# The last two late slots of a mixture-of-experts kernel as one mixed slot, and the third walk's first weights behind two conditional loads

## The chip, the cores and the metric

The kernel runs on one core of a Trainium2 chip. The metric is the device time of one execution in microseconds, the median of several runs. Of the engines, TensorE (PE) multiplies, VectorE (DVE) and ScalarE (ACT) work on the results, GpSimd (POOL) issues gathers and scatters, and SyncE (SP) issues loads and transposes by DMA, one after the other from one queue.

## The reference

Three stages run one after the other on 4608 tokens of width 512.

```python
k_p, v_p = k, v averaged over groups of 8 keys          # 8 batches, 8 heads, 576 queries, 72 keys
attn = softmax(scale * q @ k_p.T) @ v_p
h = x @ w_in                                            # 512 -> 2048
x = (max(h, 0) + alpha * min(h, 0)) @ w_out             # 2048 -> 512
expert = argmax(x @ w_gate)                             # 8 experts, one for each token
out[t] = gate[t] * (max(x[t] @ w1[e], 0) @ w2[e])       # e = expert[t], 512 -> 1024 -> 512
```

The tokens of an expert are known only at run time. With the inputs of this case the experts hold 537, 0, 1152, 576, 615, 576, 576 and 576 tokens.

## The kernel before

Float32 products are made of 16-bit parts: each operand is split into a high and a low half, and three matmuls (high·high, high·low, low·high) stand for one product. The operations of the first stages and of most of the last are given to a planner with a key (a due time) each; it fixes one order for each engine by keys, by which operation must wait for which, and by buffers that are taken and given back. The order is then written out as it stands.

The expert stage works in *slots* of up to 128 tokens of one expert. Slots 0 to 7 (the A slots) take tokens known early, 8 and up (the B slots) the rest. A slot goes through these steps: `tok` (ScalarE reads a row number into a register and loads the slot's token list, L1517), `gather` (GpSimd fetches the token rows, L1527), `xT` (SyncE transposes them, L1540), the first product `s1t` (24 matmuls of 512 columns, line `hp` L1561), ReLU on ScalarE (`rlt`), the split on VectorE (`hst`), two transposes on SyncE (`hT`, L1577), the second product `s2t` (24 matmuls, L1584), scaling on VectorE (`fin`, L1606 and L1608) and a scatter on GpSimd (`scat`, L1611).

The weights of a slot are held in one of three sets of buffers, the *walks*: A slots alternate between walks 0 and 1, B slots go over walks 0, 2, 1. `wload` (L1503 to L1511) issues a slot's weights on SyncE: `wload(0)` reads one or two registers and issues the pair of loads for the first product, `wload(1)` the pair for the second, 1 MB each. They are conditional: a slot whose walk already holds its expert skips the transfer, but the instructions stay in the queue. The first loads of a walk (slots 0, 1 and 9) are unconditional. Those of slot 9, the first on walk 2, wait in the plan for `oXt[5]`, the transpose of slot 5's tokens.

How many B slots there are is known only at run time; 31 with these inputs, so slot 38 is the last. Slots up to 36 are planned in full. From slot 37 on (`cond` = 38, `n >= cond - 1`) a slot's functions are kept in `tail`, and `run_tail` writes them out behind the plan, inside branches on the number of slots. These slots use `s1` (96 matmuls with the weights stationary and 128 token columns moving, L1552), whose result needs no transpose, and `s2` (48 matmuls for two slots, L1601). Slot 37's first product is still planned.

`plan_disp` sets up the tables for the B slots with small VectorE operations: `dB` (slots for each expert), `rows` and `rows2` (row numbers), `change` (which slot must load weights), `scales`.

Of the kernel before, what the change touches and what calls it, by code (L numbers as in the profile page):

```python
# [185 lines left out]
def attn_moe_moe_kernel(ctx: ExitStack, tc: tile.TileContext, q, k, v, w_in, w_out, alpha,  # L186
# [1165 lines left out]
    disp, cntA, cntB = {}, {}, {}  # L1352
    NW = (NSL - NA + 2) // 3

    def disp_0():
# [15 lines left out]
    def plan_disp(c, nm, key, o_cnt, o_c, o_inv):  # L1371
# [27 lines left out]
        def dB():  # L1399
            ni, nf, inc, off = t("ni", [128, NE], I32), t("nf", [128, NE]), t("inc", [128, NE]), t("off", [128, 1, NE])  # L1400
            V.scalar_tensor_tensor(out=nf, in0=cntA["u"], scalar=-128.0, in1=c["cp"], op0=ALU.mult, op1=ALU.add)
            V.tensor_scalar(out=ni, in0=nf, scalar1=127.0, scalar2=None, op0=ALU.add)
# [5 lines left out]
            ai, af = t("ai", [128, 2], I32), t("af", [128, 2])  # L1408
# [3 lines left out]
            V.tensor_copy(af, ai)  # L1412
            V.tensor_tensor(out=af[:, 0:1], in0=tot, in1=af[:, 0:1], op=ALU.subtract)
            V.tensor_scalar(out=jt[:, 2, :, 0], in0=jt[:, 0, :, 0], scalar1=1.0, scalar2=None, op0=ALU.add)
            V.tensor_scalar(out=jt[:, 1, :, 0], in0=jt[:, 2, :, 0], scalar1=af[:, 1:2], scalar2=None, op0=ALU.add)
            V.tensor_scalar(out=jt[:, 0, 1:, 0], in0=jt[:, 0, 1:, 0], scalar1=af[:, 0:1], scalar2=None, op0=ALU.add)
            V.tensor_copy(c["tot"], tot)
# [9 lines left out]
        def rows2():  # L1427
# [7 lines left out]
            if is_a:  # L1435
                V.scalar_tensor_tensor(out=regs[:, 0, :], in0=ej[:, :, 0], scalar=float(NT), in1=oj[:, :, 0],
                                       op0=ALU.mult, op1=ALU.add)
                return
            V.scalar_tensor_tensor(out=oj, in0=ej, scalar=float(NT), in1=oj, op0=ALU.mult, op1=ALU.add)
            oh, uj = t("oh", [128, n2, NE]), t("uj", [128, n2, 1])  # L1440
# [5 lines left out]
            V.scalar_tensor_tensor(out=regs[:, 0, :], in0=uj[:, :, 0], scalar=128.0, in1=oj[:, :, 0],  # L1446
                                   op0=ALU.mult, op1=ALU.add)

        def change():
# [10 lines left out]
        def scales():  # L1460
# [8 lines left out]
            V.tensor_tensor(out=ge, in0=c["oh"], in1=disp["wi"].to_broadcast([128, n2, NE]), op=ALU.mult)  # L1469
            V.tensor_reduce(out=sj, in_=ge, axis=AX.X, op=ALU.add)  # L1470

        o = counted[NB - NLAST] = add("PE", 0.1, count, [o_cnt], key=key, acq=[("gps", 1)])
        o = add("DVE", tiny(5 if is_a else 15), dA if is_a else dB, [o, o_c], key=key, rel=[("gps", 1)])
        o_w = add("DVE", tiny(4), rows, [o], key=key)
        o_r = add("DVE", tiny(5 if is_a else 10), rows2, [o_w], key=key)
        o_ch = add("DVE", tiny(2 if is_a else 5), change, [o_w], key=key + 0.1)
        o_s = add("DVE", tiny(6), scales, [o_r] + o_inv, key=key + 2)
# [4 lines left out]
    wbuf, oS1, oS2, oXt, oGa, last = {}, {}, {}, {}, {}, {}  # L1482
    tail, own = [], []

    def plan_slots(c0, lo, n_slots, oD, o_x2, o_tab, o_exp, base, cond):
# [3 lines left out]
        for i in range(n_slots):  # L1489
# [23 lines left out]

            def tok(s=s, c=c):
# [16 lines left out]
            def xT(c=c, n=n, tt=tt):  # L1531
                if n <= cond:
                    c["xT"] = wk.tile([128, 2 * KD, 128], F16, tag=tt, name="x2gT", bufs=2)
                else:
                    i = n - cond - 1
                    if i == 0:
                        own.extend(big([128, 2, 16, 128], F16, f"own{z}") for z in range(3))
                    c["ht"] = own[i // 2][:, i % 2].rearrange("p (z f) t -> p z f t", z=2)
                    c["xT"] = own[2].rearrange("p a (b f) t -> p (a b) f t", b=2)[:, i]
                Y.dma_start_transpose(out=c["xT"], in_=c["x2"])  # L1540

            def s1(f4, c=c, walk=walk):
                if "ht" not in c:
                    c["ht"] = wk.tile([128, 2, KF2, 128], F16, tag="eo", name="ht", bufs=2)
# [58 lines left out]

            def fin(s=s, c=c):
                cb = wk.tile([128, 1], F32, tag="cb", name="cb", bufs=2)
                V.tensor_tensor(out=cb, in0=c["rec"][:, 1:2], in1=c0["sj"][:, s, :], op=ALU.mult)  # L1606
                c["o"] = wk.tile([128, DM], F32, tag="q", name="so", bufs=3)
                V.tensor_scalar(out=c["o"], in0=c["op"], scalar1=cb, scalar2=None, op0=ALU.mult)  # L1608
# [4 lines left out]

            if n >= cond - 1:
                tail.append(((tok, gather, xT), wload, s1, rl, hs, s2, fin, scat))
            if n >= cond + 3:
                continue
            late = n == cond + 2
            d1 = d2 = []
# [10 lines left out]
            o_w1 = add("SP", 0.01 if rare else dmat(1 << 21), lambda f=wload: f(0), [o_w] + o_exp + d1, key=key - 14, acq=got)  # L1630
            if not late:
                o_w2 = add("SP", 0.01 if rare else dmat(1 << 21), lambda f=wload: f(1), [o_w1] + o_exp + d2, key=key - 13, acq=got)
            if n > cond + 1:
                continue
            if n == cond + 1:
# [5 lines left out]

            if n >= cond:
                continue
            hl = []
            if n < cond - 1:
                for f4 in range(KF2 // 4):
# [5 lines left out]
                    hl.append(add("SP", 1.0, lambda f=hT, f4=f4: f(f4), [o], order=hl[:], kind="xT", key=key - 20,  # L1652
                                  acq=[(th, 1)] if f4 == 0 else [], rel=[(tl, 1)]))
                o = oS2[n] = add("PE", pe(24, DM), s2t, hl + [o_w2], key=key + SLAG, acq=[("y", 1)], rel=[(th, 1)])
# [3 lines left out]
            for f4 in range(KF2 // 4):  # L1658
                o = oS1[n, f4] = add("PE", pe(48, 128), lambda f=s1, f4=f4: f(f4), [o_x, o_w1, oS1.get((n, f4 - 1))],
                                     key=key - 4.2 + 2 * f4, acq=[("h", 1)] + ([("eo", 1)] if f4 == 0 else []),  # L1660
                                     rel=[(tt, 1)] if f4 == KF2 // 4 - 1 else [])
                o = add("ACT", act(512), lambda f=rl, f4=f4: f(f4), [o], key=key - 2 + 2 * f4, acq=[("e", 1)], rel=[("h", 1)])
                hl.append(add("DVE", 0.5 + dve(512), lambda f=hs, f4=f4: f(f4), [o], key=key - 1 + 2 * f4, rel=[("e", 1)]))

    def run_tail():
# [3 lines left out]

        def up(k):  # L1670
            s1, rl, hs = tail[k][2:5]
            for f4 in range(KF2 // 4):
                s1(f4)
                rl(f4)
                hs(f4)

        def down(k):
            for f in tail[k][5:]:
                f()

        def step(k):
# [3 lines left out]
            with tc.If(total > NSL - NA - nt + 1 + k) as cmp:  # L1685
                if k + 3 < nt:
                    for f in tail[k + 3][0]:
                        f()
                up(k + 1)
                if k + 4 < nt:  # L1690
                    tail[k + 4][1](0)
                down(k)
                if k + 3 < nt:
                    tail[k + 3][1](1)
                step(k + 1)
            with cmp.Else():
                down(k)
        step(0)


# [66 lines left out]
```

## Time and profile before

| | us |
|---|---|
| three runs | 1320.1, 1323.67, 1324.22 (median 1323.67) |
| the profiled execution | 1320.55 |
| its span, first to last instruction | 1318.5 |
| mean granted TensorE clock | 0.981 |
| TensorE busy | 1266.5 (96%) |
| VectorE busy | 902.1 (68%) |
| ScalarE busy | 566.4 (43%) |
| GpSimd busy | 313.6 (24%) |

Times in rows count from the span's start. A share of busy time is a mean over all stages. The time of a matmul in a row (379 ns for 512 columns) runs from its issue to its modelled end, and matmuls overlap, so what a pass costs TensorE is the distance from its start to the next start. SPq, ACTq and POOLq are the queues in which an engine issues DMA; such a row shows how long the issue took, not the transfer. "x4" joins instructions that followed each other.

### The profile page before, as it was taken

What the parts mean: (1) busy time and instruction counts of PE and PEld (TensorE: products, weight loads), DVE (VectorE), ACT (ScalarE), POOL (GpSimd) and SP (SyncE); (2) the same over time, 40 slices, a digit from 0 to 9 for tenths busy, and PEclk for the clock granted to TensorE, in tenths of its full rate; (3) what the DMA queues carried; (4) which work ended last, traced back from release to release, by engine and by line L of the source; (5) the groups of instructions that cost most, each with busy time, mean ns of one, the idle gap of its engine ahead of it and who ended that gap; (6) DMA issues with size and microseconds to landing.
All of it is one profiled execution on the core that took longest, in us unless ns stands there. A gap on an engine that the chain in (4) does not pass through costs nothing. (4 is left out here: it accounts for less than half of the span.)

```text
span 1318.5 us, 25527 instructions
## 1 busy us (share of the span) xinstructions
PE 1266.5 (96%) x9181; PEld 785.3 (60%) x9181; DVE 902.1 (68%) x2206; ACT 566.4 (43%) x1316; POOL 313.6 (24%) x347
## 2 busy tenths in 40 slices
PE   4789999999999999999999999999989999999997
PEld 3677566677667667756776676674434444444454
DVE  4999888998999899889998887754423222323231
ACT  4887454565467447546665665431101111111110
POOL 2543432112231212123331211021121122122101
PEclk9689999999999999999999999999989999999999
DMA  9943696677788687797977665498778755999765
GB/s 269 352 123 88 164 246 161 160 196 188 168 201 196 164 200 194 162 206 199 258 201 170 181 193 154 95 310 194 221 177 196 159 128 151 253 252 210 152 191 183
DMA packets 374491, 252.64 MB, mean 192 GB/s; under 512 B 321927, under 2 KB 323095, under 8 KB 369752
## 3 DMA queue, kind: packets, MB, share of 16 engines
q1 hardware_dynamic: 360904, 230.67, 70.1%
q0 software_dynamic: 7552, 20.23, 5.0%
q8 instruction: 75, 1.23, 0.4%
q10 hardware_dynamic: 5904, 0.04, 0.3%
q14 instruction: 56, 0.46, 0.1%
HBM read 264.57 MB, written 54.87 MB: 242 GB/s over the span
## 5 line engine op out<-in xcount | busy, mean ns | idle before, releaser
L1066 PE MATMUL hp<-xT,w_in_hl 128*128 128x256 f16 x3456 | 392.4, 274 | 2.1 <-DVE r L1084 1.3
L1113 PE MATMUL yp<-w_out_hl,gT 128*128 128x512 f16 x1728 | 383.6, 379 | 1.6 <-DVE x L252 1.6
L1066 PEld LDWEIGHTS <-w_in_hl 128*128 128x128 f16 x3456 | 334.6, 98 | 46.7 <-issue 3.6
L1113 PEld LDWEIGHTS <-gT 128*128 128x128 f16 x1728 | 165.7, 98 | 192.2 <-issue 1.7
L1561 PE MATMUL hp<-ws,x2gT 128*128 128x512 f16 x888 | 199.7, 382 | 6.4 <-DMA ws<-wsc 5.5
L1566 ACT ACTIVATE hr<-hp 128x512 f32<-128x512 f32 x74 | 44.2, 597 | 324.4 <-PE hp L1561 304.0
L1561 PEld LDWEIGHTS <-x2gT 128*128 128x128 f16 x888 | 87.2, 98 | 113.2 <-DMA x2gT<-x2g 6.0
L1584 PE MATMUL op<-ws,hT 128*128 128x512 f16 x672 | 149.3, 379 | 0.0
L1084 DVE SCALAR_TENSOR_TENSOR r<-r,al,hp 128x256 f32<-128x256 f32 x288 | 123.7, 471 | 8.9 <-ACT r L1080 8.2
L1570 DVE CAST hl<-hr 128x512 f16<-128x512 f32 x74 | 31.8, 429 | 142.7 <-ACT hr L1566 137.2
L1080 ACT ACTIVATE r<-hp 128x512 f32<-128x512 f32 x144 | 86.7, 602 | 79.0 <-PE hp L1066 55.6
L749 ACT ACTIVATE e<-sc,nb,esc 128x72 f32<-128x72 f32 x256 | 103.4, 419 | 36.0 <-DVE nb L741 19.4
L1608 DVE TENSOR_SCALAR so<-op,cb 128x512 f32<-128x512 f32 x39 | 29.3, 751 | 126.7 <-PE op L1584 112.3
L1584 PEld LDWEIGHTS <-hT 128*128 128x128 f16 x672 | 65.6, 98 | 78.9
L1527 POOL DMA_INDIRECT x2g<-x2d,srec x41 | 42.8, 1045 | 271.8 <-issue 147.4
L1092 ACT ACTIVATE gT<-r 128x512 f16<-128x512 f32 x138 | 87.7, 636 | 39.5 <-DVE r L1084 21.7
L237 ACT ACTIVATE eo<-ew,es 128x512 f16<-128x512 f32 x120 | 84.1, 725 | 41.4 <-DMA wsc<-eo 16.6
L1097 DVE TENSOR_TENSOR gT<-r,gT 128x512 f16<-128x512 f32 x128 | 92.0, 723 | 2.1 <-ACT gT L1092 1.4
L1255 POOL DMA_INDIRECT table<-rec,pu x36 | 44.5, 1235 | 201.7 <-DMA table<-rec,pu 45.0
L252 DVE SCALAR_TENSOR_TENSOR eo<-ew,es,eo 128x512 f16<-128x512 f32 x107 | 80.0, 759 | 2.5 <-ACT eo L237 2.2
L232 DVE TENSOR_REDUCE em<-ew 128x1 f32<-128x1024 f32 x64 | 76.6, 1207 | 3.7 <-DMA ew<-in_moe_w_dram 3.7
L520 DVE TENSOR_REDUCE kp<-raw 72x64 f32<-72x512 f32 (+2 forms) x62 | 66.5, 1074 | 4.0 <-DMA raw<-in_v_dram 3.2
(271 smaller groups left out, 1358.2 us busy)
## 6 DMA issues: line engine op xcount, KB each, us to landing
ws<-wsc SPq DMA_DIRECT2D x166, 1024.0 KB
ew<-in_moe_w_dram SPq DMA_DIRECT2D x32, 1024.0 KB
wsc<-eo SPq DMA_DIRECT2D x64, 512.0 KB
x2d<-x SPq DMA_DIRECT2D x36, 256.0 KB
qr<-in_q_dram SPq DMA_DIRECT2D x32, 256.0 KB
w_in_f<-in_moe_w_in_dram SPq DMA_DIRECT2D x16, 512.0 KB
w_out_f<-in_moe_w_out_dram SPq DMA_DIRECT2D x16, 512.0 KB
raw<-in_v_dram SPq DMA_DIRECT2D x56, 144.0 KB
```

The source lines that it names most:

```text
L232: V.tensor_reduce(out=o, in_=i, axis=axis, op=ALU.max, apply_absolute_value=True)
L237: A.activation(out=hi, in_=src, func=ACTF.Copy, scale=s)
L252: V.scalar_tensor_tensor(out=lo, in0=src, scalar=s, in1=hi, op0=ALU.mult, op1=ALU.subtract)
L749: A.activation(out=c["e"][x], in_=c["scv"][x], func=ACTF.Exp, bias=c["nb"][:, z // 4, z % 4:z % 4 + 1], scale=c["esc"], accum_out=c["sm"][x])
L1066: T.matmul(out=hp, lhsT=wt[:, a, kk, (m % 4) * 128:(m % 4 + 1) * 128], rhs=xTt[j][:, x, kk, :], start=(n == 0), stop=(n == 3 * KD - 1))
L1080: A.activation(out=c["r"], in_=hps[j, m // 2], func=ACTF.Relu, scale=-1.0)
L1084: V.scalar_tensor_tensor(out=c["r"][:, z], in0=c["r"][:, z], scalar=al1[:, m - 1 + z:m + z], in1=hps[j, m // 2][:, z], op0=ALU.mult, op1=A ...
L1092: A.activation(out=gT[j][0][:, n2], in_=c["r"], func=ACTF.Copy)
L1097: on(eng).tensor_tensor(out=gT[j][1][:, n2], in0=c["r"], in1=gT[j][0][:, n2], op=ALU.subtract)
L1113: T.matmul(out=ypt[i], lhsT=gT[j][x][:, m, o_ * 128:(o_ + 1) * 128], rhs=W["w_out"][part][:, w, m % 4, :], start=(m == 0 and x == 0 and w ...
L1561: T.matmul(out=hp, lhsT=c["xT"][:, x * KD + kk, :], rhs=ws[kk // 2][:, kk % 2, a, 512 * f4:512 * f4 + 512], start=(kk == 0 and x == 0 and ...
L1584: T.matmul(out=op, lhsT=c["hT"][:, f // 4, 4 * x + f % 4, :], rhs=ws[f // 4][:, f % 4, w, :], start=(f == 0 and x == 0 and w == 0), stop=( ...
```

## The change

There are two parts. First, slots 37 and 38 are done as one *mixed* slot when two conditions hold: each of the two has at most 64 tokens left, and the B slots number 31. `mixed` computes this flag and the row at which the second half's token list begins. Then `tok` of slot 37 loads two lists of 64 tokens, one for each half of the partitions (without the flag they are the two halves of slot 37's own list). In the branch on the flag the tail does `s1m` (for each 128 hidden units 12 matmuls with one expert's weights and 64 token columns, then 12 with the other's and the other 64), the planned slot's second product, and `s2m` (48 matmuls, the two experts' alternating, each with 64 stationary columns and its own half of the output partitions). Without the flag the tail goes as before, with one more slot in it: slots from 36 on are now finished in the tail, and slot 37's first product is no longer planned. Slots beyond the last repeat its expert.

Second, the first loads of walk 2 wait for the conditional first loads of slots 6 and 7 (`oW1[6]`, `oW1[7]`) in place of `oXt[5]`.

```diff
+        def mixed():
+            x, v, f = t("xm", [128, 2, NE]), t("vm", [128, 2, 1]), t("fm", [128, 2])
+            flag, row, sm = t("flag", [128, 1], I32), t("row", [128, 1], I32), t("sm", [128, 1])
+            r0, r1 = (c["regs"][:, 0, m:m + 1] for m in MIX)
+            V.tensor_tensor(out=x, in0=c["oh"][:, MSEL], in1=c["rem"].to_broadcast([128, 2, NE]), op=ALU.mult)
+            V.tensor_reduce(out=v, in_=x, axis=AX.X, op=ALU.add)
+            V.tensor_tensor(out=v, in0=v, in1=c["om"], op=ALU.subtract)
+            V.tensor_reduce(out=f[:, 0:1], in_=v, axis=AX.XY, op=ALU.max)
+            V.tensor_scalar(out=f[:, 0:1], in0=f[:, 0:1], scalar1=64.0, scalar2=None, op0=ALU.is_le)
+            V.tensor_scalar(out=f[:, 1:2], in0=c["inc"][:, NE - 1:NE], scalar1=float(COND - NA + 1), scalar2=None, op0=ALU.is_equal)
...
+                if n == COND - 1:
+                    row2 = A.value_load(c0["row"][0:1, 0:1], min_val=0, max_val=TROWS - 64)
+                    A.dma_start(out=c["rec"][0:64], in_=table[bass.ds(row, 64), :])
+                    A.dma_start(out=c["rec"][64:128], in_=table[bass.ds(row2, 64), :])
+                    return
...
+            def s1m(f4, c=c, walks=(walk, other)):
...
+                for f in range(4):
+                    ff = f4 * 4 + f
+                    for w, h in zip(walks, half):
+                        z = 0
+                        for kk in range(KD):
+                            for a, x in ((0, 0), (0, 1), (1, 0)):
+                                T.matmul(out=hp[:, f, h], lhsT=wbuf[w, 0][kk // 2][:, kk % 2, a, ff * 128:(ff + 1) * 128],
+                                         rhs=c["xT"][:, x * KD + kk, h], start=(z == 0), stop=(z == 3 * KD - 1))
+                                z += 1
+
+            def s2m(c=c, walks=(walk, other)):
+                c["op"] = op = ps_y.tile([128, DM], F32, tag="y", name="op")
+                for f in range(KF2):
+                    for x, w in ((0, 0), (0, 1), (1, 0)):
+                        for v, h in zip(walks, half):
+                            T.matmul(out=op[h], lhsT=c["ht"][:, x, f, h], rhs=wbuf[v, 1][f // 4][:, f % 4, w, :],
+                                     start=(f == 0 and x == 0 and w == 0), stop=(f == KF2 - 1 and x == 1))
...
             if first_w and n >= NA:
-                d1 = d2 = [oXt[NA - 3]]
+                d1, d2 = [oW1[NA - 2]], [oW1[NA - 1]]
...
+        mix = nc.values_load(cntB["flag"][0:1, 0:1], min_val=0, max_val=1)
+        with tc.If(mix > 0) as cmp:
+            up(1, 8)
+            down(0)
+            tail[1][9]()
+            tail[1][6](mix=True)
+            tail[1][7]()
+        with cmp.Else():
+            body(0)
```

SyncE's queue of before, around the first loads of walk 2 (`ws0_2` is the first product's weights on walk 2, `ws1_2` the second's; `regsA` is read for slots 0 to 7, `regsB` for later ones; `ws0_0` behind the second register read is slot 6's):

```order
L1511 DMA ws1_1_12466<-wsc_78 128x4096
L1503 TENSOR_LOAD regsB_175
...
L1511 DMA ws0_2_12945<-wsc_78 128x4096
...
L1577 DMA_TRANSPOSE hT_12990<-hl_12971 128x8x128
L1540 DMA_TRANSPOSE x2gT_12997<-x2g_12659 128x8x128
L1577 DMA_TRANSPOSE hT_12990<-hl_12994 128x8x128
L1503 TENSOR_LOAD regsA_170
...
L1511 DMA ws0_0_12340<-wsc_78 128x4096
...
L1511 DMA ws1_2_13049<-wsc_78 128x4096
```

The same place of the changed kernel, from the same conditional load on:

```order
L1541 DMA ws1_1_12466<-wsc_78 128x4096
L1576 DMA_TRANSPOSE x2gT_12993<-x2g_12659 128x8x128
L1613 DMA_TRANSPOSE hT_13000<-hl_12975 128x8x128
...
L1541 DMA ws0_0_12340<-wsc_78 128x4096
...
L1541 DMA ws0_1_12393<-wsc_78 128x4096
...
L1613 DMA_TRANSPOSE Abuf0_99<-hl_13114 128x8x128
L1533 TENSOR_LOAD regsB_175
...
L1541 DMA ws0_2_13179<-wsc_78 128x4096
...
L1541 DMA ws1_2_13309<-wsc_78 128x4096
```

`ws0_2` has moved from ahead of three transposes and slot 6's first weights to behind slot 7's (`ws0_1`), and `ws1_2` has moved with it, to behind the second weights of slots 4 and 5, which stand in the part left out.

TensorE's list of before at the end of the plan (the last matmul of slot 36's second product, then the tail's first product for slot 38):

```order
L1584 MATMUL op_16713<-ws1_2_13050,hT_16490 128x512
L1667 TENSOR_LOAD totB_174
L1685 COMPARE_AND_BRANCH
L1552 LDWEIGHTS ws0_0_12340
L1552 MATMUL hp2_16788<-x2gT_16329,ws0_0_12340 128x128
```

And of the changed kernel (the last matmul of slot 35's second product, then the mixed first product, slot 36's second product and the mixed second product; without buffer numbers on some names):

```order
L1620 MATMUL op<-ws_0_12424,hT 128x512
L1722 TENSOR_LOAD totB
L1757 TENSOR_LOAD flagB
L1758 COMPARE_AND_BRANCH
L1653 LDWEIGHTS ws_1_12393
L1653 MATMUL hp_16661<-x2gT,ws_1_12393 128x64
...
L1620 MATMUL op<-ws_2_13310,hT 128x512
L1662 LDWEIGHTS ht
L1662 MATMUL op<-ws_1_12465,ht 64x512
L1662 LDWEIGHTS ht
L1662 MATMUL op<-ws_0_12423,ht 64x512
```

The branch now comes one slot earlier in the list, with one more register read, and behind it 192 matmuls of 64 columns, 24 of 512 and 48 of 512 with half the stationary columns.

## Rows read from the trace of the kernel before

**Rows 1.** TensorE's waits: line waited for: us in total, times, longest.

```profile
PE hp L1561 <- DMA ws<-wsc: 5.5, 1, 5.5
```

**Rows 2.** Timeline of TensorE: start, us, engine, line, operation, count, [idle before <-releaser].

```profile
944.40 5.34 PE L1561 MATMUL hp<-ws,x2gT 128*128 128x512 f16 x24 [0.90 <-issue]
...
960.41 7.82 PE L1561 MATMUL hp<-ws,x2gT 128*128 128x512 f16 x24 [5.49 <-DMA ws<-wsc]
968.06 5.34 PE L1584 MATMUL op<-ws,hT 128*128 128x512 f16 x24
...
999.14 5.34 PE L1584 MATMUL op<-ws,hT 128*128 128x512 f16 x24
```

**Rows 3.** Windows: stretch, length, busy (instructions) by engine, granted clock, DMA share, GB/s.

```profile
928.00:934.00 6.00, 6.00 (x29) 2.74 (x28) 4.26 (x15) 1.19 (x2) 1.06 (x1) 1.00 0.65 111
...
956.00:960.00 4.00, 0.00 (x0) 0.00 (x0) 0.00 (x0) 0.00 (x0) 0.00 (x0) 0.83 0.81 152
960.00:964.00 4.00, 3.59 (x9) 1.35 (x10) 0.00 (x0) 0.00 (x0) 1.03 (x1) 0.50 0.53 111
964.00:968.00 4.00, 4.00 (x16) 1.63 (x15) 1.30 (x2) 0.60 (x1) 1.97 (x2) 0.82 1.09 216
```

**Rows 4.** Timeline of SyncE's queue in the same stretch.

```profile
930.79 2.26 SPq L1511 DMA_DIRECT2D ws<-wsc  x4
933.15 3.86 SPq L1577 DMA_TRANSPOSE hT<-hl  x1
...
944.32 1.48 SPq L1511 DMA_DIRECT2D ws<-wsc  x4
945.88 10.04 SPq L1577 DMA_TRANSPOSE Abuf<-hl  x2
...
956.93 1.24 SPq L1540 DMA_TRANSPOSE x2gT<-x2g  x1
960.22 0.45 SPq L1511 DMA_DIRECT2D ws<-wsc  x2
...
993.88 0.56 SPq L1511 DMA_DIRECT2D ws<-wsc  x2
...
1001.49 0.53 SPq L1511 DMA_DIRECT2D ws<-wsc  x2
```

**Rows 5.** Timeline of all engines, the last 50 us.

```profile
1270.45 0.15 DVE L1606 TENSOR_TENSOR cb<-srec,sjB 128x1 f32<-128x1 f32 x1
...
1273.68 5.52 PE L1552 MATMUL hp<-x2gT,ws 128*128 128x128 f16 x96
...
1279.04 15.70 PE L1584 MATMUL op<-ws,hT 128*128 128x512 f16 x72
...
1294.58 5.52 PE L1552 MATMUL hp<-x2gT,ws 128*128 128x128 f16 x96
...
1299.94 10.52 PE L1601 MATMUL op<-ws,ht 128*128 128x512 f16 x48
...
1306.26 1.93 SPq L1511 DMA_DIRECT2D ws<-wsc  x4
...
1310.50 0.75 DVE L1608 TENSOR_SCALAR so<-op,cb 128x512 f32<-128x512 f32 x1 [4.36 <-PE op L1601]
1311.89 0.99 POOL L1611 DMA_INDIRECT out_dram<-so,srec  x1 [4.53 <-DVE so L1608]
```

**Rows 6.** Timeline of TensorE around short attention passes.

```profile
311.14 0.68 PE L730 MATMUL sc<-KTb,qT 128*128 128x72 f16 x16
311.66 0.17 PE L1231 MATMUL rp<-oh,tri 128*128 128x8 bf16 x1
...
850.77 0.66 PE L789 MATMUL xp<-AT,VSb 128*64 128x128 f16 x16
851.36 0.82 PE L1113 MATMUL yp<-w_out_hl,gT 128*128 128x512 f16 x3
```

**Rows 7.** Chain that ended last: start, us, what.

```profile
1306.35 4.76 DMA out_dram<-so,srec
```

**Rows 8.** Page, groups of instructions: busy, mean ns of one, idle before.

```profile
L1561 PEld LDWEIGHTS <-x2gT 128*128 128x128 f16 x888 | 87.2, 98 | 113.2 <-DMA x2gT<-x2g 6.0
```

More of the change, by code (lines that the diff above doesn't have):

```diff
@@ L1353, in attn_moe_moe_kernel @@
     NW = (NSL - NA + 2) // 3
+    MIX = [((n - NA) % 3) * NW + (n - NA) // 3 for n in (COND, COND - 1)]
+    MSEL = slice(MIX[0], MIX[1] + 1, MIX[1] - MIX[0])
     def disp_0():
@@ L1447, in rows2 @@
                                    op0=ALU.mult, op1=ALU.add)
+        def mixed():
[8 more added lines that the diff above has]
+            V.tensor_scalar(out=f[:, 1:2], in0=c["inc"][:, NE - 1:NE], scalar1=float(COND - NA + 1), scalar2=None, op0=ALU.is_equal)
+            V.tensor_tensor(out=f[:, 0:1], in0=f[:, 0:1], in1=f[:, 1:2], op=ALU.mult)
+            V.tensor_copy(flag, f[:, 0:1])
+            V.scalar_tensor_tensor(out=f[:, 1:2], in0=r1, scalar=64.0, in1=r0, op0=ALU.add, op1=ALU.subtract)
+            V.tensor_tensor(out=f[:, 1:2], in0=f[:, 1:2], in1=f[:, 0:1], op=ALU.mult)
+            V.scalar_tensor_tensor(out=row, in0=r1, scalar=64.0, in1=f[:, 1:2], op0=ALU.add, op1=ALU.subtract)
         def change():
@@ L1470, in scales @@
             V.tensor_reduce(out=sj, in_=ge, axis=AX.X, op=ALU.add)
+            if not is_a:
+                V.tensor_copy(c["sm"][0:64], sj[0:64, MIX[1]])
+                V.tensor_copy(c["sm"][64:128], sj[64:128, MIX[0]])
         o = counted[NB - NLAST] = add("PE", 0.1, count, [o_cnt], key=key, acq=[("gps", 1)])
-        o = add("DVE", tiny(5 if is_a else 15), dA if is_a else dB, [o, o_c], key=key, rel=[("gps", 1)])
+        o = add("DVE", tiny(5 if is_a else 19), dA if is_a else dB, [o, o_c], key=key, rel=[("gps", 1)])
         o_w = add("DVE", tiny(4), rows, [o], key=key)
         o_r = add("DVE", tiny(5 if is_a else 10), rows2, [o_w], key=key)
+        if not is_a:
+            o_r = add("DVE", tiny(11), mixed, [o_r], key=key)
         o_ch = add("DVE", tiny(2 if is_a else 5), change, [o_w], key=key + 0.1)
-        o_s = add("DVE", tiny(6), scales, [o_r] + o_inv, key=key + 2)
+        o_s = add("DVE", tiny(6 if is_a else 8), scales, [o_r] + o_inv, key=key + 2)
         if is_a:
@@ L1480, in plan_disp @@
         return o_w, o_r, o_ch, o_s
-    wbuf, oS1, oS2, oXt, oGa, last = {}, {}, {}, {}, {}, {}
+    wbuf, oS1, oS2, oXt, oGa, oW1, last = {}, {}, {}, {}, {}, {}, {}
     tail, own = [], []
@@ L1537, in xT @@
                         own.extend(big([128, 2, 16, 128], F16, f"own{z}") for z in range(3))
+                    c["own"] = True
                     c["ht"] = own[i // 2][:, i % 2].rearrange("p (z f) t -> p z f t", z=2)
@@ L1542, in s1 @@
             def s1(f4, c=c, walk=walk):
-                if "ht" not in c:
+                if f4 == 0 and "own" not in c:
                     c["ht"] = wk.tile([128, 2, KF2, 128], F16, tag="eo", name="ht", bufs=2)
@@ L1602, in s2, with fin @@
                                  start=(f == 0 and x == 0 and w == 0), stop=(f == KF2 - 1 and x == 1))
-            def fin(s=s, c=c):
+            half = (slice(0, 64), slice(64, 128))
+            other = (0, 2, 1)[(i + 1) % 3]
+            def s1m(f4, c=c, walks=(walk, other)):
+                if f4 == 0 and "own" not in c:
+                    c["ht"] = wk.tile([128, 2, KF2, 128], F16, tag="eo", name="ht", bufs=2)
+                c["hp", f4] = hp = ps_h.tile([128, 4, 128], F32, tag="h", name="hp2")
+                for f in range(4):
[14 more added lines that the diff above has]
+                                     start=(f == 0 and x == 0 and w == 0), stop=(f == KF2 - 1 and x == 1))
+            def fin(s=s, c=c, mix=False):
                 cb = wk.tile([128, 1], F32, tag="cb", name="cb", bufs=2)
-                V.tensor_tensor(out=cb, in0=c["rec"][:, 1:2], in1=c0["sj"][:, s, :], op=ALU.mult)
+                V.tensor_tensor(out=cb, in0=c["rec"][:, 1:2], in1=c0["sm"] if mix else c0["sj"][:, s, :], op=ALU.mult)
                 c["o"] = wk.tile([128, DM], F32, tag="q", name="so", bufs=3)
@@ L1612, in scat @@
                                      in_=c["o"], in_offset=None, bounds_check=NT - 1, oob_is_err=False)
-            if n >= cond - 1:
-                tail.append(((tok, gather, xT), wload, s1, rl, hs, s2, fin, scat))
-            if n >= cond + 3:
+            if n >= cond - 2:
+                tail.append(((tok, gather, xT), wload, s1, rl, hs, s2t if n == cond - 2 else s2, fin, scat, s1m, s2m))
+            if n >= cond + 2:
                 continue
-            late = n == cond + 2
+            late = n == cond + 1
             d1 = d2 = []
@@ L1629, in plan_slots @@
             rare = not first_w
-            o_w1 = add("SP", 0.01 if rare else dmat(1 << 21), lambda f=wload: f(0), [o_w] + o_exp + d1, key=key - 14, acq=got)
+            o_w1 = oW1[n] = add("SP", 0.01 if rare else dmat(1 << 21), lambda f=wload: f(0), [o_w] + o_exp + d1, key=key - 14, acq=got)
             if not late:
                 o_w2 = add("SP", 0.01 if rare else dmat(1 << 21), lambda f=wload: f(1), [o_w1] + o_exp + d2, key=key - 13, acq=got)
-            if n > cond + 1:
-                continue
             if n == cond + 1:
@@ L1640, in plan_slots @@
             oXt[n] = o_x
-            if n >= cond:
+            if n >= cond - 1:
                 continue
@@ L1653, in plan_slots @@
                                   acq=[(th, 1)] if f4 == 0 else [], rel=[(tl, 1)]))
+                if n == cond - 2:
+                    continue
                 o = oS2[n] = add("PE", pe(24, DM), s2t, hl + [o_w2], key=key + SLAG, acq=[("y", 1)], rel=[(th, 1)])
@@ L1657, in plan_slots @@
                 continue
[L1658 to L1663, printed above, removed]
     def run_tail():
@@ L1668, in run_tail, with up @@
         nt = len(tail)
-        def up(k):
-            s1, rl, hs = tail[k][2:5]
+        def up(k, i=2):
+            s1, rl, hs = tail[k][i], *tail[k][3:5]
             for f4 in range(KF2 // 4):
@@ L1677, in down, with body @@
         def down(k):
-            for f in tail[k][5:]:
+            for f in tail[k][5:8]:
                 f()
+        def body(k):
+            if k and k + 3 < nt:
+                for f in tail[k + 3][0]:
+                    f()
+            up(k + 1)
+            if k + 4 < nt:
+                tail[k + 4][1](0)
+            down(k)
+            if k + 3 < nt:
+                tail[k + 3][1](1)
+            step(k + 1)
         def step(k):
@@ L1685, in step @@
             with tc.If(total > NSL - NA - nt + 1 + k) as cmp:
[L1686 to L1695, printed above, removed]
+                body(k)
             with cmp.Else():
                 down(k)
-        step(0)
+        mix = nc.values_load(cntB["flag"][0:1, 0:1], min_val=0, max_val=1)
[7 more added lines that the diff above has]
+            body(0)
     tile0 = {b: min(i for i in range(NTL) if any(x[2] == b for x in segs(i))) for b in range(B)}
```

19 lines of the change are left out of this document (13 added, 6 removed).

## The prediction

> **What bounds the kernel now.** I read four views in this order: the waits of TensorE, its timeline around the longest wait, the SyncE timeline of the same stretch, and the timeline of the last 50 us. The waits say that from the slots of the expert stage only one wait is long: a first product that stood 5.49 us for a weight transfer [rows 1]. Everywhere else in that stage TensorE goes from one pass of 24 matmuls to the next: passes start 5.18 us apart, so a slot of two passes costs 10.36 us, and what counts is TensorE's own work plus the places where it stands.
>
> The stand is at the start of the late slots [rows 2]. First product of slot 6 starts at 944.40 after 0.90 us of idle, first product of slot 7 at 960.41 after 5.49 us. That second pass takes 7.65 us to the next start (960.41 to 968.06) in place of 5.18, which is 2.47 us more: the granted clock had gone to 0.50 in 960 to 964, with TensorE idle through all of 956 to 960, and came back within 964 to 968 [rows 3]. Together 0.90 + 5.49 + 2.47 = 8.9 us are lost there.
>
> Why it stood is on SyncE's queue [rows 4]. Slot 7's first weights are the pair of conditional loads at 960.22, 0.2 us before the matmul. They are late since the queue in front of them is long: two 2 MB loads for the third walk go out at 930.79 and 944.32 (each in one group with a conditional pair), and the transposes right behind each are slow: one of 3.86 us, and two that take 10.04 us together. One at 956.93 takes 1.24 us. SyncE works through this list without a long pause until slot 7's second weights at 993.88.
>
> At the end, TensorE's last work is [rows 5]: first product of slot 37 (96 matmuls, 5.36 us to the next start), second products of slots 34, 35, 36 (72, 15.54 us), first product of slot 38 (5.36), second products of slots 37 and 38 (48, 10.52), end at 1310.46. No gap between them, although a branch is crossed. From there to the end of the span are 8.0 us: the scaling, the scatter, its landing.
>
> **The third walk's loads move (stage start).** The first pair of the third walk goes behind slot 7's first conditional load, the second pair further back, as the two SyncE pieces of the order show. So the loads at 930.79 and 944.32 no longer stand ahead of the first weights of slots 6 and 7. Taking the 2 MB loads and the slow transposes behind them away (3.86 − 1.24 for one, 10.04 − 2.48 for the two) frees over 10 us on SyncE ahead of 960.22, and slot 7 needs 5.7 of it: both waits go, with the slow clock behind them: −8.9 us on that spot.
>
> What is late next: the same SyncE list, in another order, stands ahead of slot 7's second weights, which SyncE reached at 993.88. Its length is about unchanged, since the two loads and two groups of slow transposes are still in it, now later; SyncE does not get there earlier than about 992 to 995. Without the stall, slot 7's second product would start at 999.14 − 8.9 = 990.2. So it would wait 2 to 5 us there; I take 3.4. Each stand of that length hits one pass only, since what follows on SyncE (slot 8's second weights at 1001.49, 7.6 us after slot 7's [rows 4], are needed 10.36 us after them) has room. Whether the clock falls is open: it did so in a stand of 5.49 us and not in the one of 0.90 [rows 2, 3]. So the stage gives 8.9 − 3.4 = 5.5 us, between 1.5 (wait 5 us, slow pass of 2.47 again) and 8.9 (SyncE early enough). The third walk's own weights come in time: slot 9, the first to use them, comes two slots, 20.7 us, behind slot 7 on TensorE, and its load right behind slot 7's.
>
> **The routing arithmetic.** Some 21 more small VectorE operations stand between the count of tokens and the slot tables. One of that size takes 0.15 us [rows 5], so 3 to 4 us on VectorE, which was busy 4.26 of 6 us in that stretch [rows 3]. Only what delays slot 4's split or the tables of the late slots could count; TensorE is two passes ahead there. Cost 0, at most 1 us if it pushes SyncE's first transposes back.
>
> **The last two slots as one.** Removed: 2 × 5.36 of first products and 10.52 of two second products, 21.2 us. Added: one mixed first product of 192 matmuls with 64 moving columns, and one mixed second product of 48 matmuls of 512 columns whose stationary side is 64 wide, the two halves alternating.
>
> First product: a matmul of 128 columns took 5.36/96 = 55.8 ns. The nearest row is the attention pass of 72 columns with a full 128 × 128 stationary operand, 16 in 0.52 us to the next start, 32.5 ns each [rows 6]. For 64 columns I take 31 ns: 192 × 31 = 5.9 us, gain 4.8. The ends: half of 55.8 ns (5.4 us, gain 5.4) if time goes by columns alone, 55.8 ns (10.7 us, no gain) if the shorter row gains nothing.
>
> The Trainium skill speaks against this: "TensorE: Matmul & The Clock Gate", section "Back-to-back issue gap", says that in a stream of load and matmul pairs both set the spacing, about 81 ns at 128 columns, and its section on LDWEIGHTS gives a load by its columns, by which 128 would take 107 ns. By that load the mixed product would be 20.5 us, 9.8 more than what it replaces. The trace has 55.8 and 32.5 ns with full loads, so it does not agree.
>
> Second product: if the two column halves run side by side, 24 pairs. The row that shows such pairs is the attention output, 64-wide stationary, 128 columns: 16 in 0.59 us to the next start, 37 ns each against 55.8 for a full one [rows 6], so a pair costs 74 ns, 18 more than one alone, and that with entry and exit in it. 24 × (5.18/24 + 0.010) = 5.4 us, gain 5.1. Ends: 10.4 us (gain 0) if 512-column halves run one behind the other, 5.2 (gain 5.3) with perfect overlap.
>
> Both: 4.8 + 5.1 = 9.9 us. The halves' split into hi and lo lies beside slot 36's second product, which stands between the two mixed passes. Two register loads and a branch come ahead of the mixed product; that before had one load and a branch and no gap at 1294.58, so 0.
>
> **The very end.** Before, four weight loads were issued at 1306.26 [rows 5] for slots that don't exist, beside the last scatters; they are not reached in the new branch. The scatter was issued at 1311.89 and one like it took 4.76 us to land [rows 7], near the end of the span at 1318.5, so the loads decide little: −0.4 us, from 0 to −2.
>
> **Sum**: −5.5 − 9.9 − 0.4 = −15.8 us. The profiled execution took 1320.55 (span 1318.5 and 2.05 outside it), so it becomes 1304.7; taken from the median of 1323.67 it is 1307.9. The profiled one lay low among the three (1320.1 to 1324.2), so I say 1306.5. About 0.3%, 4 us, is what a measurement here can tell from no change.
>
> **Rivals.**
> 1. *The whole stall moves to slot 7's second product* (or slot 6's): wait about 5 us and the slow clock again. For it: SyncE is the long queue, and its list is not shorter. Against: the end needed at 990.2 is only 2 to 5 us ahead. Gain 1.5 + 10.3: 1308.8 by the profile, about 1311.
> 2. *All stalls vanish*: SyncE reaches 993.88's pair 4 us earlier since transposes behind the moved loads are quicker (3.86 us in one case and 5.0 in the other [rows 4], so it varies). Gain 8.9 + 10.3: 1301.4, about 1303.
> 3. *One half of the tail fails*: halves one behind the other, or the first product tied to its weight loads. The loads' own duration is 98 ns [rows 8]; at 55.8 ns each the first product gains nothing. Gain 5.5 + 5: about 1313; with both, 1318.
> 4. *The branch isn't taken* (one of the two experts over 64 tokens left, or another slot total). Slot 38 ran in the trace, so the total fits; from the inputs I count 576 tokens for each of the two experts, 64 over full slots. Only the stage's 5.5 is left: 1318.
> 5. *Slower*: the loads of the third walk now fall amid slots that run at TensorE's pace, and SyncE's delay does not end with one slot. If four passes in a row wait 4 us each and run at the low clock (2.47 more), 26 us stand against 8.9 removed and 10.3 of the tail: 7 us worse, 1330. It decides from the point where SyncE reaches slot 7's second weights 15 us or more later than 993.88. Against: the list is no longer than before, and with that list the slots after 968 ran without one wait.
>
> **Numbers.** Forecast 0.55, rival 1 0.15, rival 2 0.14, rival 3 0.08, rival 4 0.03, slower 0.05. Faster by over 0.3%: the forecast, rivals 1 and 2 and most of 3 and 4, 0.91; within: the rest of 3 and 4 and part of 5, 0.05; slower: 0.04. The likeliest one's own range is 1303 to 1310; to 1298 for rival 2 with a low median, to 1317 for rivals 1 and 3.
>
> **What would show it.** In the timeline of TensorE: no idle ahead of the first products of slots 6 and 7, one of 2 to 5 us ahead of slot 7's second product (none: rival 2; over 5 with a clock of 0.5: rival 1; several: rival 5). On SyncE: slot 7's first pair some 15 us earlier, its second pair still near 993. In the tail: 192 matmuls in 5.9 us and 48 in 5.4; 10.7 or 10.4 there is rival 3; a group of 96 matmuls of 128 columns is rival 4. The forecast is wrong if the time is over 1317 or if the tail's two groups sum to over 16 us.

## The result, and the profile after

| | before | changed |
|---|---|---|
| median | 1323.24 us (1320.1 to 1324.22, 4 runs) | 1308.25 us (1304.71 to 1311.46, 4 runs) |
| ratio, 95% interval | | 0.9894, 0.9863 to 0.9925 |
| profiled execution's span | 1318.5 us | 1304.5 us |
| end of TensorE's last pass to the end of the span | 8.0 us | 7.05 us |

The change makes the kernel 15 us faster by the medians, 14 by the ratio; 1306.5 was forecast, in a range of 1298 to 1317.

The 14.0 us between the two profiled spans come from four places. First the timeline of TensorE of the changed kernel, over the slots where the kernel before stood still.

```profile
942.28 5.34 PE L1597 MATMUL hp<-ws,x2gT 128*128 128x512 f16 x24
...
952.64 5.34 PE L1597 MATMUL hp<-ws,x2gT 128*128 128x512 f16 x24
...
979.32 5.35 PE L1620 MATMUL op<-ws,hT 128*128 128x512 f16 x24 [0.61 <-DMA ws<-wsc]
...
993.40 8.24 PE L1620 MATMUL op<-ws,hT 128*128 128x512 f16 x24 [3.55 <-DMA ws<-wsc]
1001.48 5.34 PE L1597 MATMUL hp<-ws,x2gT 128*128 128x512 f16 x24
```

The first products of slots 6 and 7 (942.28 and 952.64) have no idle before them, where [rows 2] had 0.90 and 5.49 us. In their place the second products of slots 6 and 7 (979.32 and 993.40) wait, 0.61 and 3.55 us. The pass behind the longer wait takes 8.08 us to the next start, 2.9 over the 5.18 of a full-speed pass. The windows (length, then busy us of PE, PEld, DVE, ACT and POOL with their instructions, granted clock, DMA share, GB/s) show why:

```profile
988.00:992.00 4.00, 1.85 (x9) 0.65 (x7) 2.28 (x5) 0.60 (x1) 0.00 (x0) 1.00 1.02 341
992.00:996.00 4.00, 2.60 (x7) 0.95 (x8) 0.00 (x0) 0.00 (x0) 0.00 (x0) 0.56 1.25 176
996.00:1000.00 4.00, 4.00 (x13) 1.42 (x12) 0.00 (x0) 0.00 (x0) 1.03 (x1) 0.59 0.48 114
```

TensorE was idle for over half of 988 to 992 and a third of 992 to 996, and the granted clock is 0.56 and 0.59 from 992 on, as it was after the longer stand before [rows 3]. An idle in a row counts from the modelled end of the pass ahead, 0.16 us past the start that the next one could have had. Counted by starts, the ten passes from slot 6's first product to slot 11's first take 1001.48 − 942.28 = 59.2 us, 7.4 over the 51.8 of ten undisturbed ones. Before they took 59.9, with 0.90 of idle ahead of them: 9.0 over. So the start of the late slots gave back only 1.6 us. Another 1.2 us is that TensorE arrives at slot 6 earlier (942.28 against 944.40 − 0.90); the executions differ by more than that before the stage, so it is not put down to the change.

SyncE's queue of the changed kernel, from slot 6's first weights (936.95) to slot 7's second (993.19):

```profile
936.95 0.45 SPq L1541 DMA_DIRECT2D ws<-wsc  x2
...
944.64 0.45 SPq L1541 DMA_DIRECT2D ws<-wsc  x2
...
947.96 1.81 SPq L1541 DMA_DIRECT2D ws<-wsc  x4
...
952.73 4.93 SPq L1613 DMA_TRANSPOSE hT<-hl  x1
...
962.90 1.64 SPq L1541 DMA_DIRECT2D ws<-wsc  x4
...
966.73 6.91 SPq L1613 DMA_TRANSPOSE hT<-hl  x1
...
988.05 4.78 SPq L1613 DMA_TRANSPOSE hT<-hl  x1
993.19 0.56 SPq L1541 DMA_DIRECT2D ws<-wsc  x2
```

Slot 7's first pair goes out at 944.64, 15.6 us earlier than the 960.22 of [rows 4]. The two 2 MB loads of walk 2 now go out with the groups at 947.96 and 962.90, and soon behind each stands a slow transpose, of 4.93 and of 6.91 us. The transpose at 988.05 takes 4.78 us, behind slot 11's first weights, which are a real transfer too. Slot 7's second pair is issued at 993.19, where before it was 993.88: SyncE gets there at about the same time, with TensorE now there sooner.

The tail, all engines:

```profile
1270.84 10.52 PE L1620 MATMUL op<-ws,hT 128*128 128x512 f16 x48
...
1281.20 5.76 PE L1653 MATMUL hp<-x2gT,ws 128*128 128x64 f16 x192
...
1286.80 5.34 PE L1620 MATMUL op<-ws,hT 128*128 128x512 f16 x24
...
1292.08 5.37 PE L1662 MATMUL op<-ws,ht 128*64 128x512 f16 x48
...
1297.49 0.75 DVE L1669 TENSOR_SCALAR so<-op,cb 128x512 f32<-128x512 f32 x1 [4.49 <-PE op L1662]
1299.99 0.99 POOL L1672 DMA_INDIRECT out_dram<-so,srec  x1 [5.80 <-issue]
```

In [rows 5] TensorE needed 36.8 us from the start behind slot 33's second product (1273.68) to its last end at 1310.46; here 26.6, from 1270.84 to 1297.45. The gain of 10.2 us is the mixed slot: 192 matmuls in 5.60 us (1281.20 to 1286.80) and 48 in 5.37. Behind it the last scatter is issued 1.75 us after the scaling ended, where it was 0.64 before, but the end comes 1.0 us sooner all the same.

### The profile page after: what moved, and what is told of

Its sections match the earlier page's. It is cut to its first block, busy times and chain, and to the rows that moved or that the text cites. A ratio compares the mean times of both kernels' runs of the same rounds, so it can differ in the third digit from the quotient of the medians.

```text
span 1304.5 us, 25485 instructions
## 1 busy us (share of the span) xinstructions
PE 1255.8 (96%) x9181; PEld 778.1 (60%) x9181; DVE 900.3 (69%) x2218; ACT 564.8 (43%) x1314; POOL 307.9 (24%) x345
## 5 line engine op out<-in xcount | busy, mean ns | idle before, releaser
L1066 PEld LDWEIGHTS <-w_in_hl 128*128 128x128 f16 x3456 | 334.6, 98 | 45.2 <-issue 3.8
L1620 PE MATMUL op<-ws,hT 128*128 128x512 f16 x672 | 152.4, 384 | 4.2 <-DMA ws<-wsc 4.2
```

The lines of the kernel that those rows point to most:

```text
L1066: T.matmul(out=hp, lhsT=wt[:, a, kk, (m % 4) * 128:(m % 4 + 1) * 128], rhs=xTt[j][:, x, kk, :], start=(n == 0), stop=(n == 3 * KD - 1))
L1620: T.matmul(out=op, lhsT=c["hT"][:, f // 4, 4 * x + f % 4, :], rhs=ws[f // 4][:, f % 4, w, :], start=(f == 0 and x == 0 and w == 0), stop=( ...
```

## The experiments

The theory: the tail gives about 10 us by itself, and the moved loads give little, since the wait only moves down SyncE's list, to slot 7's second weights, and takes the low clock with it. The rivals are in the expectations.

**The moved loads alone.** The kernel before with this edit (and the line that keeps the operations in `oW1`):

```diff
-                d1 = d2 = [oXt[NA - 3]]
+                d1, d2 = [oW1[NA - 2]], [oW1[NA - 1]]
```

> Only the second part of the change: walk 2's first loads wait for the first loads of slots 6 and 7; routing arithmetic, planned end and tail as before. Theory (the stall moves from slot 7's first product to slot 7's second product, since SyncE's list in front of that pair is as long as before): no idle before the first products of slots 6 and 7; a wait of 2 to 5 us at slot 7's second product, a slow pass of about 2.9 us more if the wait is over 3 us, slot 7's second weights issued near 993; 1 to 3 us faster than before, tail of 21.2 us unchanged. Rival (the stage gives 5 us or more when the extra VectorE arithmetic is not there): slot 7's second weights issued by 990, no wait, 6 to 9 us faster.

Measured: median 1321.62 us against 1323.55, ratio 0.9987 (0.9956 to 1.0017), which is no change clear of the spread. TensorE and the granted clock around slot 7's second product, and the tail:

```profile
995.54 7.03 PE L1584 MATMUL op<-ws,hT 128*128 128x512 f16 x24 [3.20 <-DMA ws<-wsc]
1002.41 5.34 PE L1561 MATMUL hp<-ws,x2gT 128*128 128x512 f16 x24
```

```profile
996.00:1000.00 4.00, 4.00 (x12) 1.44 (x11) 0.00 (x0) 0.00 (x0) 1.03 (x1) 0.58 0.57 119
```

```profile
1292.66 5.52 PE L1552 MATMUL hp<-x2gT,ws 128*128 128x128 f16 x96
1298.03 10.76 PE L1601 MATMUL op<-ws,ht 128*128 128x512 f16 x48
```

3.20 us of idle and a pass of 6.87 us (1.7 over) make 4.9 lost where the kernel before lost 8.9; TensorE's tail is the old one. The theory's wait is there without the added arithmetic, and the rival's 6 to 9 us are not. The slow pass cost 1.7 us where about 2.9 was expected.

The end of this trace shows something more:

```profile
1307.43 1.93 SPq L1511 DMA_DIRECT2D ws<-wsc  x4
...
1309.85 0.99 POOL L1611 DMA_INDIRECT out_dram<-so,srec  x1 [4.40 <-DVE so L1608]
```

```profile
1312.00:1314.00 2.00, 0.00 (x0) 0.00 (x0) 0.00 (x0) 0.00 (x0) 0.00 (x0) 0.85 1.01 418
```

The four weight loads for slots that don't exist go out as in [rows 5], and after TensorE and the issue of the last scatter are done, DMA still moves 418 GB/s. TensorE's last end is at 1308.78 and the span ends at 1319.9: 11.1 us, where the same tail took 8.0 in the trace of the kernel before. All nine traces with the mixed slot, where these loads are not reached, have 7.0 to 7.3. So the old end was 1 us longer than the new one in one trace and 4 in the other; that the loads make it so is likely, but no run changed them alone.

**The mixed slot alone.** The changed kernel with this line put back:

```diff
-                d1, d2 = [oW1[NA - 2]], [oW1[NA - 1]]
+                d1 = d2 = [oXt[NA - 3]]
```

> Only the first part of the change: the mixed slot with its arithmetic; walk 2's first loads wait for slot 5's tokens as before. Theory (the tail gives the gain, by itself): the mixed products take 5.6 and 5.4 us, about 10.2 us less than slot 37 and 38 took, 1 us more at the end; idle of about 5.5 us before slot 7's first product and the slow pass behind it are there again (8 to 9 us lost); 10 to 12 us faster than before. Rival (the two parts need each other: without the moved loads the added arithmetic makes the start of the slots worse): idle before the first products of slots 6 and 7 over 9 us together, 5 us faster or less.

Measured: median 1314.69 us against 1323.55, ratio 0.9919 (0.9886 to 0.9951), 8.9 us in the medians and 10.7 by the ratio of 1323.55. TensorE at slot 7's first product and in the tail:

```profile
959.83 8.20 PE L1597 MATMUL hp<-ws,x2gT 128*128 128x512 f16 x24 [6.03 <-DMA ws<-wsc]
967.87 5.34 PE L1620 MATMUL op<-ws,hT 128*128 128x512 f16 x24
```

```profile
1283.85 6.07 PE L1653 MATMUL hp<-x2gT,ws 128*128 128x64 f16 x192
1289.76 5.34 PE L1620 MATMUL op<-ws,hT 128*128 128x512 f16 x24
1295.03 5.37 PE L1662 MATMUL op<-ws,ht 128*64 128x512 f16 x48
```

6.03 us of idle and 2.86 of the slow pass are 8.9 lost, as before the change; there is no wait at slot 6. The mixed products take 5.9 and 5.4 us. So the added arithmetic on VectorE costs TensorE nothing there. By the ratios the two parts alone give 1.7 and 10.7 us, and together 14.0; the difference is within the spread, so neither needs the other, and the 1.7 is not clear of no change.

**Slot 7's second weights earlier in the queue.** The changed kernel; `oW2` keeps the operations of the second weights, and parts of the lines are left out:

```diff
-            o_w1 = oW1[n] = add("SP", ..., [o_w] + o_exp + d1, key=key - 14, acq=got)
+            o_w1 = oW1[n] = add("SP", ..., [o_w] + o_exp + d1, order=[oW2[7]] if n == 11 else [], key=key - 14, acq=got)
...
-                    hl.append(add("SP", 1.0, ..., [o], order=hl[:], kind="xT", key=key - 20,
+                    hl.append(add("SP", 1.0, ..., [o], order=hl[:] + ([oW2[7]] if n == 8 and f4 else []), kind="xT", key=key - 20,
```

> The changed kernel with an order on SyncE: slot 7's second weights go ahead of slot 8's second transpose, and slot 11's first weights (a real transfer) behind it. Nothing else differs. Theory (slot 7's second product waits for its place in SyncE's list and nothing else; the low clock follows from that wait): the wait of 3.55 us at slot 7's second product and the 2.90 us of the slow pass go; the 0.6 us at slot 6's second product stays; slot 11's first weights are issued 4 us later, near 987, and its first product may wait up to 3 us; 3.5 to 6.5 us faster than the changed kernel, 1302 to 1305. Rival (SyncE falls behind in any order, the wait only moves on): the sum of waits and slow passes between 970 and 1020 stays near 7 us, at slot 11's first or slot 8's second product, time as the changed kernel.

Measured: median 1306.46 us against 1323.55, ratio 0.986 (0.9806 to 0.9913). Its only stand in the stage:

```profile
985.94 5.35 PE L1620 MATMUL op<-ws,hT 128*128 128x512 f16 x24 [1.69 <-DMA ws<-wsc]
```

```profile
984.00:988.00 4.00, 2.31 (x12) 0.99 (x11) 1.49 (x4) 0.60 (x1) 2.06 (x2) 1.00 0.89 183
```

The waits and slow passes are 1.7 us in place of 7.1 (0.61, 3.55 and 2.90), and the granted clock stays at 1.00. But the median was only 1.8 us under the changed kernel's, where 3.5 to 6.5 was expected; the two came from different comparisons, and this trace reaches slot 6's first product 5.6 us later (947.83 against 942.28). So this kernel, the next one and the changed one were run side by side.

> The changed kernel once more, beside the two reordered ones below on the same chip, so that all three have the same kernel of before next to them. Theory: 0.989 of the time before, 13 to 15 us less; in the profile 0 to 1 us at slot 6's second product, 2 to 4 us at slot 7's, and a slow pass where the second wait is over 3 us. Rival (the earlier runs of it were favourable): 0.993 or more.

The changed kernel: median 1311.28 us (1308.7 to 1315.43) against 1322.82, ratio 0.9905 (0.9875 to 0.9934).

```profile
983.02 5.35 PE L1620 MATMUL op<-ws,hT 128*128 128x512 f16 x24 [0.75 <-DMA ws<-wsc]
...
997.92 8.22 PE L1620 MATMUL op<-ws,hT 128*128 128x512 f16 x24 [4.37 <-DMA ws<-wsc]
1005.98 5.34 PE L1597 MATMUL hp<-ws,x2gT 128*128 128x512 f16 x24
```

0.75 and 4.37 us of idle and a pass of 8.06 us, 2.9 over: 8.0 us lost. The second wait is a little over the expected 2 to 4.

> The same kernel as in the run with slot 7's second weights moved ahead. Its profile lost 1.7 us between slots 6 and 8 in place of 7.1, and its median was 1.8 us under the changed kernel's of another chip and hour. Theory (the 5.4 us are real and the medians differ by the chip and by what happens in the first 90 us): 3 to 6 us faster than the changed kernel in this comparison. Rival (TensorE's wait there is covered later, so that it does not count in the time): within 1.5 us of the changed kernel.

Slot 7's second weights first: median 1304.26 us (1300.7 to 1307.71), ratio 0.9857 (0.983 to 0.9885), 7.0 us under the changed kernel beside it, more than the 3 to 6 expected. TensorE, and SyncE's queue in which the pair at 984.72 is slot 7's second and the one at 988.71 slot 11's first:

```profile
979.76 5.35 PE L1620 MATMUL op<-ws,hT 128*128 128x512 f16 x24 [0.34 <-DMA ws<-wsc]
...
990.14 5.34 PE L1620 MATMUL op<-ws,hT 128*128 128x512 f16 x24
...
997.30 4.04 PE L1597 MATMUL hp<-ws,x2gT 128*128 128x512 f16 x18 [0.53 <-DMA ws<-wsc]
```

```profile
948.51 1.81 SPq L1541 DMA_DIRECT2D ws<-wsc  x4
...
984.72 0.52 SPq L1541 DMA_DIRECT2D ws<-wsc  x2
...
988.71 0.99 SPq L1541 DMA_DIRECT2D ws<-wsc  x2
```

From the load group at 948.51 to slot 7's second weights are 36.2 us; in the changed kernel it was 45.2 (947.96 to 993.19). Slot 7's second product does not wait; 0.34 us at slot 6's and 0.53 within slot 11's first product are left. That is 0.9 us lost against 8.0 beside it, 7.1 less, and the medians differ by 7.0: the loss in the stage counts in full. The rivals, that the wait only moves on or is covered later, fall: what moved on is half a microsecond.

**Walk 2's second load later.** The changed kernel with one dependency replaced:

```diff
-                d1, d2 = [oW1[NA - 2]], [oW1[NA - 1]]
+                d1, d2 = [oW1[NA - 2]], [oW2[NA - 1]]
```

> The changed kernel, with the second pair of walk 2's first loads (2 MB) behind slot 7's second weights instead of slot 7's first. Theory (the transposes behind that pair, 2.0 and 6.9 us, are what puts SyncE behind): slot 6's and slot 7's second weights are issued 4 to 6 us earlier, both waits (0.61 and 3.55 us) and the slow pass (2.90) go; what is behind the pair now is late instead: slot 8's second weights come near 1000 to 1004 and slot 8's second product waits 0 to 4 us; 3 to 7 us faster than the changed kernel. Rival (the transposes are slow for another reason than this pair): hT of 5 us or more still stands near 966, slot 7's second weights near 993, no gain.

Measured: median 1302.41 us against 1323.55, ratio 0.9821 (0.9767 to 0.9876). Its trace has no wait of TensorE in the stage either.

> The same kernel as in the run with the second pair of walk 2's loads behind slot 7's second weights; its profile had no wait at all between slots 6 and 13. Theory: 5 to 8 us faster than the changed kernel in this comparison, the 7 us of waits and slow pass; no wait at slots 6, 7 and 8 in the profile. Rival: within 1.5 us of the changed kernel, or a wait at slot 8's second product in this profile.

Side by side with the two above: median 1301.35 us (1300.06 to 1303.5), ratio 0.9829 (0.9802 to 0.9855), 9.9 us under the changed kernel, where 5 to 8 was expected, and the fastest of all. TensorE from slot 6's second product to slot 7's, and SyncE's queue:

```profile
980.11 5.34 PE L1620 MATMUL op<-ws,hT 128*128 128x512 f16 x24
985.28 5.34 PE L1597 MATMUL hp<-ws,x2gT 128*128 128x512 f16 x24
990.47 5.34 PE L1620 MATMUL op<-ws,hT 128*128 128x512 f16 x24
```

```profile
964.24 0.52 SPq L1541 DMA_DIRECT2D ws<-wsc  x2
...
966.27 1.52 SPq L1613 DMA_TRANSPOSE hT<-hl  x1
...
973.76 0.53 SPq L1541 DMA_DIRECT2D ws<-wsc  x2
...
986.37 1.68 SPq L1541 DMA_DIRECT2D ws<-wsc  x4
...
992.72 4.37 SPq L1613 DMA_TRANSPOSE Abuf<-hl  x1
```

Every pass starts within 0.02 us of 5.18 after the one before, with no idle at either place. The pair at 964.24 is now slot 5's second weights alone; the transpose after the next takes 1.52 us where it took 6.91, slot 6's second weights go out at 973.76 and slot 7's with the group at 986.37, ahead of walk 2's 2 MB. The slow transpose is there again, 4.37 us at 992.72, behind that load, where no wait of TensorE follows. So the slowness belongs to the load and not to the place, and the rival falls; the expected wait at slot 8's second product did not come either. 9.9 us in the medians is more than the 8.0 that the changed kernel's profile lost in this comparison; the other 2 us are within the spread of the runs and were not followed.

**The mixed second product without alternation.**

```diff
-                for f in range(KF2):
-                    for x, w in ((0, 0), (0, 1), (1, 0)):
-                        for v, h in zip(walks, half):
+                for v, h in zip(walks, half):
+                    for f in range(KF2):
+                        for x, w in ((0, 0), (0, 1), (1, 0)):
```

> The changed kernel, with the mixed second product's two halves one after the other (24 matmuls of one expert, then 24 of the other) in place of alternating; same 48 matmuls. Theory (the gain of this product is that two 64-wide halves run side by side, and only when neighbours in the list use different halves): 48 matmuls in about 10.4 us in place of 5.37, TensorE's end 5 us later. Rival (a matmul with half the stationary columns is simply quicker by itself): 5.4 us as before.

One execution, 1320.93 us against 1323.19. TensorE's list, slots 34 and 35's second products and the mixed one:

```profile
1280.72 10.52 PE L1620 MATMUL op<-ws,hT 128*128 128x512 f16 x48
...
1302.27 9.71 PE L1662 MATMUL op<-ws,ht 128*64 128x512 f16 x48
```

The group takes 9.71 us in place of 5.37. Most of its matmuls start 216 ns after one another, as full-width ones do, so a half-wide matmul alone is no quicker; the halves run side by side only where both stand close together in the list. The 0.8 us under the 10.52 of 48 full-width matmuls [rows 5] are four pairs around the change of halves, with starts 6 to 30 ns apart. The semaphores in the trace tell the halves apart there: the second half's first matmul, told by the wait that it carries, starts at 1306.62, and the first half's last one, which signals, at 1307.26. So TensorE started matmuls of the second half ahead of the last three of the first. The rival falls. This one execution reached the tail late: slot 34's second product starts at 1280.72, 9.9 us later than in the changed kernel's trace (1270.84), so its time as a whole says little.

**The mixed first product with fewer columns.**

```diff
-                                T.matmul(out=hp[:, f, h], ..., rhs=c["xT"][:, x * KD + kk, h], ...
+                                g = slice(h.start, h.start + (64 if z == 0 else 32))
+                                T.matmul(out=hp[:, f, g], ..., rhs=c["xT"][:, x * KD + kk, g], ...
```

> The changed kernel, with 32 token columns in place of 64 in 11 of 12 matmuls of the mixed first product (half of each expert's tokens are left out of those sums, so its output is not the reference's); the loads of the stationary weights are the same 192. Theory (at 64 columns the columns set the pace, 29.2 ns where half of 55.8 is 27.9, with a floor near the 25 ns of the gate's 16-column matmuls): 192 matmuls in 4.8 to 5.1 us in place of 5.60. Rival 1 (the weight loads set the pace): 5.6 us, no change. Rival 2 (no floor, time goes by columns alone): about 3.1 us.

One execution, 1314.29 us against 1323.19. TensorE:

```profile
1289.62 2.24 PE L1654 MATMUL hp<-x2gT,ws 128*128 128x64 f16 x82
1292.20 2.95 PE L1654 MATMUL hp<-x2gT,ws 128*128 128x32 f16 x110 [0.33 <-issue]
1294.99 5.34 PE L1620 MATMUL op<-ws,hT 128*128 128x512 f16 x24
```

A row joins matmuls of both widths and names one of them; 176 of the 192 have 32 columns. 1289.62 to 1294.99 is 5.37 us, with one break in the middle, a step of 0.51 us between two starts, for which the profile shows no cause (`issue`). Behind it 110 matmuls start in 2.79 us (1292.20 to 1294.99), 25.4 ns each against 29.2 at 64 columns, so without the break the product takes 4.9 us, as the theory has it. The loads of the weights, as many as before, do not set 29.2 ns. The columns alone do not set 25.4, since half of them saved 13%, and rival 2 falls; what sets it is not shown. Rival 1 said no change from 5.60; as measured it is off by 0.2 us only, so it falls by the steps and not by the total.

## Why the prediction was right, and the step that was not

- **What bounds the kernel.** Right: both losses named were in TensorE's list, and 11.8 of the 14.0 us between the profiled spans came out of the two places.
- **The moved loads.** The waits at the first products of slots 6 and 7 went, slot 7's first pair came 15.6 us earlier (about 15 was said), SyncE reached its second pair at 993.19 (992 to 995), and slot 7's second product waited 3.55 us (2 to 5, 3.4 taken). The step that failed is the next: "8.9 − 3.4 = 5.5 us" counted no slow pass, with "whether the clock falls" left open. It fell: 2.90 us, and 0.6 to 0.8 us at slot 6's second product, which was not foreseen at all. The stage gave 1.6 us, the price of rival 1 (1.5), not of the forecast.
- **The mixed slot.** Forecast 5.9 and 5.4 us, measured 5.60 and 5.37; gain 9.9 against 10.2. The nearest rows [rows 6] were good prices, 32.5 ns at 72 columns for 29.2 at 64, so the forecast was right to go by them. For the second product the sum took 10 ns more for a pair where its row gave 18; pairs start 216 ns apart, as single full-width matmuls do, so nothing was to be added. The Trainium skill ("TensorE: Matmul & The Clock Gate", section on LDWEIGHTS) gives 107 ns for such a load by its formula; as a pace of loads the trace does not agree, with 192 of them in 5.60 us.
- **The arithmetic.** Nothing, as said, though the change adds 18 small operations and not 21; in the trace the tables take 3.15 us more of VectorE, within the 3 to 4 said. In the run with the mixed slot alone the loss at slot 7 is 8.9, as before.
- **The very end.** 1.0 in place of 0.4, within its bounds. That the four loads "decide little" is not borne out: with the same tail the run with the moved loads alone needed 11.1 us there, against 7.0 to 7.3 with the mixed slot, so the term may be 4, outside the 0 to 2 said.
- **The sum.** 15.8 was said for the profiled execution, 14.0 is measured: 3.9 too much in the stage, 0.3 and 0.6 too little in the tail and at the end, and 1.2 that came from ahead of the stage. So that 1306.5 is within 2 us of 1308.25 is in part luck: the smaller terms made up for more than half of the stage's.

## What to carry to other kernels

When a load moves away from one wait, count the queue that issues it up to the next thing the busy engine needs: here the same 2 MB loads stood behind a wait of 5.5 us in the one place, of 3.55 in the next, and of none once the second one came after all that was needed soon. Price a wait of TensorE with the slow pass that follows it, 1.7 to 2.9 us after stands of 3.2 us and more. Two half-empty slots can share one: 64 columns in place of 128 cost about half (29.2 against 55.8 ns), though 32 in place of 64 saved only 13%, and half-wide stationary operands run in pairs if they alternate in the list.

## What the runs showed of the hardware

- Stands of 0.3 to 1.7 us within the slots left the granted clock at 1.00; stands of 3.20, 3.55, 3.96, 4.08, 4.37, 5.49 and 6.03 us each came with a stretch at 0.5 (1.2 GHz in place of 2.4), and the pass behind them took 6.86 to 8.08 us in place of 5.18. No stand between 1.7 and 3.2 us occurred there.
- Transposes on SyncE's queue behind a 2 MB load took up to 6.95 us in place of 1.24, and the slow ones moved with the load wherever it was put.
- Pairs of matmuls with 64 stationary columns each and 512 moving ones ran at the price of one: 48 in 5.37 us to their modelled end, against 5.34 for 24 of full width. With the halves one after the other they took 9.71, and around the change of halves four pairs still formed, out of the order of the list.
- With a full 128 x 128 load ahead of every matmul, starts were 216 ns apart at 512 moving columns, 55.8 at 128, 29.2 at 64 and 25.4 where most had 32.
- The same kernel's mixed first product took 5.60 us in one execution and 5.9 in another; the difference is one step of 0.33 to 0.35 us between two starts, for which the profile shows no cause.
